# An H3-convolution and linear-attention kernel: the inverse 16-point stage by stationary products, u turned by DMA, denominators spread through DRAM

## The chip, the cores and the metric

The kernel runs on one core of a Trainium2 chip. The metric is the device time of one execution in microseconds (us), quoted as the median of several runs. The profile's span, from the first to the last instruction of the core, is about 2 us shorter. Engines are named as the profile does: PE (TensorE, matmuls), PEld (its weight loads), DVE (VectorE), ACT (ScalarE), POOL (GpSimd), SP (SyncE, which issues the DMAs here). SBUF and PSUM are the core's two on-chip memories: here matmuls write to PSUM, and an eviction is the copy of a result from there to SBUF. A turn is a transpose. A run is called slow when it is over 1.5% above the fastest run of the same kernel; some runs of about half the versions here are, the kernel before's too. Ratios and intervals use fast runs only, medians all runs.

## The reference

Two independent blocks share the output, 576 columns each, for S = 2048 rows, D = 576 and bf16 data. This is the reference cut to what matters.

```python
def A(q, k, v, shift_k, ssm_k, ssm_D):                       # H3 convolution
    kv = causal_conv_4_taps(k, shift_k) * v                  # called u in the kernel
    y  = irfft(rfft(kv padded to 2S) * rfft(ssm_k padded))[:S]
    y  = bf16(y) + kv * ssm_D
    return q * y

def B(x, wqkv, wo):                                          # linear attention, 32 heads of 18
    q, k, v = heads(x @ wqkv)
    phi = lambda t: where(t > 0, t + 1, exp(t)) + 1e-6
    num = phi(q) @ (phi(k)^T v)
    den = phi(q) . sum(phi(k)) + 1e-6
    return merge(num / den) @ wo

return concatenate([A, B], -1)
```

The kernel does the long convolution as a two-level transform: a 128-point stage with a table `Gsb`, a 16-point stage with small constant matrices, a product of the two spectra, an inverse 16-point stage, and an inverse 128-point stage with a table `Esb`. The 576 channels are worked in 9 groups of 64.

## The kernel before

Every operation is recorded with what it reads and writes. A fixed string, `PLAN`, then gives each operation's engine (P, A, D, G for GpSimd, S) and the order of issue, and another string, `PLACES`, gives the address of every tile. So the order on each engine and the sharing of memory are decided by these strings.

The inverse 16-point stage of one group. `X` is the spectrum of the filter with real and imaginary rows exchanged; the two products overwrite `xb` and `tx`. Small constant weights (64 x 64 tiles) are stationary and the products move, 512 columns a matmul; the result `V` is then turned by a DMA.

```python
load("X", xb, lambda e: dma(xb.t[0:128:2], tx.t[1:128:2]), ...)       # and the odd rows
P.op({"DVE":..., "POOL":...},                                         # the plan chooses the engine
     lambda e: vec(e).tensor_tensor(out=xb.t[:], in0=su.t[:], in1=xb.t[:], op=ALU.mult), name="p2")
P.op({"DVE":..., "POOL":...},
     lambda e: vec(e).tensor_tensor(out=tx.t[:], in0=su.t[:], in1=tx.t[:], op=ALU.mult), name="p1")
for jp in range(2):
    for wi, (w, src) in enumerate(((W31, tx), (W32, xb))):
        for h in range(2):
            for g2 in range(2):
                v = src.t[64*h:64*h+64].rearrange("p (w g) k -> p g w k", g=2)
                nc.tensor.matmul(ps.t[64*g2:64*g2+64, h, :]..., lhsT=w()[64*h:64*h+64, :],
                                 rhs=v[:, g2, 4*jp:4*jp+4, :], start=(wi == 0), stop=(wi == 1))
    copy(e, V.t[:, :, 4*jp:4*jp+4, :]..., ps.t)                       # eviction
turn("Vtr", Vt[hf].t[:, c0//4:c0//4+16, :], V.t[:]...)                # DMA transpose
```

The last stage (`i2`) reads `Vt` as the moving operand and multiplies the result by `q` on DVE:

```python
vt = Vt[hf].t[:].rearrange("p g (h r t) -> p r (g h) t", h=2, t=2)    # pairs of bf16, 128 bytes apart
nc.tensor.matmul(o, lhsT=Esb.t[:, b, ri, :], rhs=vt[:, 2*b+ri, :], start=(ri == 0), stop=(ri == 1))
nc.vector.tensor_tensor(out=qs, in0=ps.t..., in1=qs, op=ALU.mult)
```

The denominators: PE spreads the reciprocals of the heads over the heads' rows into PSUM, and DVE multiplies phi(q) by them.

```python
def b_bc(c, gp):
    ps = psb(2, "bps")
    for j in range(2):
        g = 2 * gp + j
        nc.tensor.matmul(ps.t[0:hn, j, :], lhsT=esel()[32*g:32*g+32, c, 0:hn],
                         rhs=rden.t[32*g:32*g+32, :], start=True, stop=True)
    nc.vector.scalar_tensor_tensor(out=o, in0=o, scalar=EPS, in1=ps.t[0:hn], op0=ALU.add, op1=ALU.mult)
```

The spectrum of u is turned by DVE in 32 x 32 blocks (`ct`, 9 times), the filter's by DMA (`ctH`, 9 times).

## Time and profile before

| | before |
|---|---|
| time, first three runs | 181.97 us median (181.44 to 182.95) |
| span | 180.0 us |
| PE idle in the span | 180.0 - 161.2 = 18.8 us |
| PE idle between 100 and 150 us | 50 - 21.16 - 23.44 = 5.4 us |
| DVE products at the spectrum, on DVE / on POOL | 13 / 5 |

From the page of the kernel before: the busy time of each engine, with its share of the span and its instructions, and the engines' shares of the chain that ended last.

```profile
PE 161.2 (90%) x1448; PEld 104.5 (58%) x1448; DVE 143.7 (80%) x136; ACT 109.8 (61%) x118; POOL 46.5 (26%) x29
...
PE 74%; DVE 9%; ACT 6%; DMA 6%; issue 2%; SPq 0%; DVEq 0%
```

PE is the limit: busy nine tenths of the span, and three quarters of the chain. The windows view of the kernel before gives, for each stretch, its length and the busy time (and count) of each engine, then the clock granted to PE, the share of the DMA engines and GB/s.

```profile
core 0: us, PE busy (x) PEld busy (x) DVE busy (x) ACT busy (x) POOL busy (x), PEclk, DMA share, GB/s
...
100.00:125.00 25.00, 21.16 (x239) 12.06 (x232) 22.00 (x20) 22.12 (x22) 13.77 (x4) 0.93 0.70 133
125.00:150.00 25.00, 23.44 (x259) 14.22 (x260) 22.05 (x21) 20.74 (x24) 8.88 (x2) 0.93 0.86 222
150.00:180.00 30.00, 26.36 (x172) 13.80 (x171) 20.47 (x21) 6.38 (x9) 0.00 (x0) 1.00 0.83 206
```

Three engines are nearly full in the middle, and from 150 us on PE alone. Groups of instructions, from the same kernel's lines view: count, busy us and mean ns, then the idle time before them and what ended it.

```profile
L782 DVE SCALAR_TENSOR_TENSOR pqT<-pqT,ps_all 126x1024 bf16<-126x1024 bf16 (+1 forms) x10 | 11.9, 1212 | 1.6 <-PE ps_all L776 1.4
...
L539 DVE TENSOR_TENSOR X<-spu,X 128x2048 bf16<-128x2048 bf16 x7 | 8.5, 1221 | 1.7 <-ACT spu L253 1.4 <-issue 0.3
L542 DVE TENSOR_TENSOR sph<-spu,sph 128x2048 bf16<-128x2048 bf16 x6 | 7.2, 1216 | 0.1
```

The end of the chain, from the same kernel's view of the chain (start, duration, engine, line, count), shows the two costs that the change is aimed at:

```profile
157.02 0.99 PE ps_all L553 x16
158.01 2.57 PE ps_all L795 x20
160.58 14.54 PE ps_all L581 x60
```

L553 is the inverse 16-point stage, 16 matmuls a group in 0.99 us; L581 is the last stage, 0.242 us a matmul (half of its 64 have 320 columns, half 256).

### The profile page before, as it was taken

To read this page: it belongs to the slowest core of one execution; us is meant where nothing else is said; L and a number is where in the kernel's file an instruction comes from. 1 tells how busy PE (TensorE), PEld (TensorE's weight loads), DVE (VectorE), ACT (ScalarE), POOL (GpSimd) and SP (SyncE) were. 2 spreads that over 40 slices of the span, in tenths; PEclk is the share of its full clock that TensorE was granted. 3 is DMA by queue.
4 is the path that set the end of the run, shared out by engine and by line. 5 is a ranking of instruction groups with operands and counts; after the bars stand their busy time and mean duration, and the time that the engine had idled before them with its cause. 6 is when DMAs were issued, how large, how long until landed. Compare 5 with 4: busy or idle time off the path is not lost.

```text
span 180.0 us, 3538 instructions
## 1 busy us (share of the span) xinstructions
PE 161.2 (90%) x1448; PEld 104.5 (58%) x1448; DVE 143.7 (80%) x136; ACT 109.8 (61%) x118; POOL 46.5 (26%) x29
## 2 busy tenths in 40 slices
PE   0795999999999979899999978788799999999991
PEld 0664677754766757676677745433348565554450
DVE  0307589898979899899969899996968999686863
ACT  2083364648856788755668889995958798620000
POOL 8004000150080340006304960653882000000000
PEclk9999799999999999999999999978969999999999
DMA  5999799999999944998096019979399983999844
GB/s 181 327 202 283 143 298 422 298 169 263 336 237 350 378 164 93 179 283 253 29 304 226 15 22 206 239 124 233 97 346 259 222 183 120 259 208 273 261 142 149
DMA packets 68886, 39.49 MB, mean 219 GB/s; under 512 B 50375, under 2 KB 66373, under 8 KB 68230
## 3 DMA queue, kind: packets, MB, share of 16 engines
q1 hardware_dynamic: 68870, 39.27, 84.9%
q8 instruction: 11, 0.18, 0.4%
q14 instruction: 5, 0.04, 0.1%
HBM read 17.77 MB, written 4.72 MB: 125 GB/s over the span
## 4 chain that ended last, share of the span: by engine, by line
PE 74%; DVE 9%; ACT 6%; DMA 6%; issue 2%; SPq 0%; DVEq 0%
PE ps_all L628 12%; PE ps_all L607 12%; PE ps_all L795 11%; PE ps_all L665 11%; PE ps_all L581 9%; PE ps_all L458 5%; PE ps_all L553 4%; PE ps_all L429 3%; DVE pqT L782 3%; DMA hs<-in_A_ssm_k_dram 3%; DMA wk<-in_B_wqkv_dram 3%; ACT Ch L253 2%; PE ps_all L508 2%; DVE Cu L255 2%; PE ps_all L501 2%
## 5 line engine op out<-in xcount | busy, mean ns | idle before, releaser
L407 POOL TENSOR_TENSOR v<-m,v 128x1536 bf16<-128x1536 bf16 x5 | 17.0, 3408 | 55.9 <-DVE m L404 26.2
L795 PE MATMUL ps_all<-M,pqT 126*128 126x288 bf16 (+1 forms) x160 | 24.3, 306 | 0.0
L253 ACT ACTIVATE sph<-ps_all 128x1024 bf16<-128x1024 f32 x18 | 18.0, 1022 | 8.4 <-PE ps_all L508 7.4
L607 PE MATMUL ps_all<-wk,xT 128*128 128x288 bf16 x128 | 21.4, 301 | 1.1 <-DMA wk<-in_B_wqkv_dram 1.1
L458 PEld LDWEIGHTS <-Gsb 128*128 128x128 bf16 x240 | 17.4, 102 | 7.4 <-issue 6.0
L396 DVE TENSOR_TENSOR m<-kh,Wj 128x3072 bf16<-128x3072 bf16 x12 | 20.8, 1748 | 0.9 <-DMA kh<-in_A_k_dram 0.9
L628 PE MATMUL ps_all<-xT,wq 128*126 128x512 bf16 (+1 forms) x80 | 20.7, 381 | 0.0
L665 PE MATMUL ps_all<-pk,x_sb 128*128 128x288 bf16 (+1 forms) x160 | 20.6, 287 | 0.0
L795 PEld LDWEIGHTS <-pqT 126*128 126x128 bf16 (+1 forms) x160 | 15.7, 103 | 8.3 <-issue 3.7
L253 ACT ACTIVATE spu<-ps_all 128x1024 bf16<-128x1024 f32 x16 | 15.8, 1026 | 4.9 <-PE ps_all L501 4.3
L665 PEld LDWEIGHTS <-x_sb 128*128 128x128 bf16 x160 | 15.3, 98 | 5.1 <-issue 1.3
L612 ACT ACTIVATE ek<-ps_all,neg 128x576 bf16<-128x576 f32 x16 | 11.8, 744 | 10.2 <-PE ps_all L607 5.3
L628 PEld LDWEIGHTS <-wq 128*126 128x126 bf16 (+1 forms) x100 | 12.7, 131 | 7.9 <-issue 0.9
L607 PEld LDWEIGHTS <-xT 128*128 128x128 bf16 x128 | 13.1, 103 | 5.5 <-issue 1.2
L581 PE MATMUL ps_all<-Vt,Esb 128*128 128x320 bf16 (+1 forms) x64 | 15.9, 421 | 0.0
L253 ACT ACTIVATE V<-ps_all 128x1024 bf16<-128x1024 f32 x13 | 12.9, 1022 | 4.1 <-PE ps_all L553 4.0
L632 ACT ACTIVATE eq<-ps_all,neg 126x1024 bf16<-126x1024 f32 (+1 forms) x10 | 11.1, 1112 | 6.4 <-PE ps_all L628 6.4
L586 DVE TENSOR_TENSOR q<-ps_all,q 128x640 bf16<-128x640 f32 (+1 forms) x12 | 11.2, 954 | 4.4 <-PE ps_all L581 4.4
L253 ACT ACTIVATE Ch<-ps_all 128x1536 bf16<-128x1536 f32 x9 | 13.0, 1501 | 1.8 <-PE ps_all L458 1.8
L615 DVE SCALAR_TENSOR_TENSOR pk<-ek,ps_all 128x576 bf16<-128x576 bf16 x16 | 11.8, 751 | 2.4 <-ACT ek L612 2.4
L635 DVE SCALAR_TENSOR_TENSOR pqT<-eq,ps_all 126x1024 bf16<-126x1024 bf16 (+1 forms) x10 | 12.2, 1215 | 1.7 <-ACT eq L632 1.5
L782 DVE SCALAR_TENSOR_TENSOR pqT<-pqT,ps_all 126x1024 bf16<-126x1024 bf16 (+1 forms) x10 | 11.9, 1212 | 1.6 <-PE ps_all L776 1.4
(77 smaller groups left out, 257.9 us busy)
## 6 DMA issues: line engine op xcount, KB each, us to landing
X<-sph SPq DMA_DIRECT2D x18, 256.0 KB, 3.9
hs<-in_A_ssm_k_dram SPq DMA_DIRECT2D x6, 384.0 KB, 4.1
v<-in_A_v_dram SPq DMA_DIRECT2D x2, 1152.0 KB, 9.6
x_sb<-in_B_x_dram SPq DMA_DIRECT2D x1, 2304.0 KB
out_dram<-ob SPq DMA_DIRECT2D x16, 144.0 KB, 3.1
kh<-in_A_k_dram SPq DMA_DIRECT2D x1, 1584.0 KB
q<-in_A_q_dram SPq DMA_DIRECT2D x1, 1280.0 KB
out_dram<-q SPq DMA_DIRECT2D x4, 320.0 KB, 2.6
```

The source lines that it names most:

```text
L253: nc.scalar.activation(out=o, in_=i, func=ACTF.Copy)
L396: nc.vector.tensor_tensor(out=m.t[:, i:i + 2], in0=i0, in1=i1, op=ALU.mult)
L407: lambda e: vec(e).tensor_tensor(out=vt.t[:, :, c0:c0 + CC], in0=m.t[:, 0], in1=vt.t[:, :, c0:c0 + CC], op=ALU.mult),
L458: nc.tensor.matmul(ps.t[:, bank, lo - 512 * bank:hi - 512 * bank], lhsT=Gsb.t[:, b, ri, :], rhs=src[:, lo - CC * j:hi - CC * j], start=Tru ...
L581: nc.tensor.matmul(o, lhsT=Esb.t[:, b, ri, :], rhs=vt[:, 2 * b + ri, :], start=(ri == 0), stop=(ri == 1))
L607: nc.tensor.matmul(ps.t[:, hh, 0:HALF], lhsT=xs(t, 128 * r, 128), rhs=wk.t[:, t, HALF * hh:HALF * hh + HALF], start=(t == 0), stop=(t == 4))
L612: P.op(("ACT", _act(576) + 0.085), lambda e: nc.scalar.activation(out=eb.t[:], in_=ps.t[:, :, 0:HALF], func=ACTF.Exp, bias=neg1.t[:]), rd= ...
L628: nc.tensor.matmul(ps.t[0:hn, j, :], lhsT=wq.t[:, t, h0:h0 + hn], rhs=xs(t, 1024 * gp + 512 * j, 512), start=(t == 0), stop=(t == 4))
L635: P.op(("DVE", _dve(1024)), lambda e: nc.vector.scalar_tensor_tensor(out=pqT.t[0:hn, c, 1024 * gp:1024 * gp + 1024].rearrange("p (h c) -> ...
L665: nc.tensor.matmul(ps.t[:, hh, 0:n], lhsT=x_sb.t[:, r, FT[t]:FT[t] + 128], rhs=pk.t[:, r, HALF * hh:HALF * hh + n], start=(r == 0), stop=( ...
L782: nc.vector.scalar_tensor_tensor(out=o, in0=o, scalar=EPS, in1=ps.t[0:hn], op0=ALU.add, op1=ALU.mult)
L795: nc.tensor.matmul(ps.t[:, hh, 0:HALF], lhsT=pqT.t[0:hn, c, 128 * r:128 * r + 128], rhs=M.t[0:hn, c, HALF * hh:HALF * hh + HALF], start=(c ...
```

## The change

The intent is to take work off PE and DVE. The products themselves become the stationary operand of the inverse 16-point stage and the constant matrix moves, so the result comes out already turned: the nine DMA turns of `V` go, and `Vt` gets a layout that the last stage reads in dense halves. The room on the DMA is used to turn u there in 7 of 9 groups (before on DVE), and to spread the denominators: the reciprocals go to DRAM once and come back as rows repeated 18 times, into a tile in SBUF. At the start, the first half of x is turned by PE (40 transposes) rather than by DMA. A new plan goes with it; it has 8 of the 18 products on POOL, before 5. The diff, cut to its core:

```diff
@@ inverse 16-point stage
-        V = SB("V", [128, 2, 8, 128])
...
-                            nc.tensor.matmul(
-                                ps.t[64 * g2:64 * g2 + 64, h, :].rearrange("p (w k) -> p w k", w=4),
-                                lhsT=w()[64 * h:64 * h + 64, :], rhs=v[:, g2, 4 * jp:4 * jp + 4, :],
-                                start=(wi == 0), stop=(wi == 1))
+                for j in range(8):
+                    for wi, src in enumerate((tx, xb)):
+                        nc.tensor.matmul(ps.t[:, j // 4, 128 * (j % 4):128 * (j % 4) + 128],
+                                         lhsT=src.t[:, 8 * jp + j, :], rhs=W3(wi), start=(wi == 0), stop=(wi == 1))
+            o0 = VN[hf] // 2 * jp + c0 // 2
+            ... copy(e, Vt[hf].t[:, :, o0:o0 + 32].rearrange("p r (j g) -> p j r g", g=4), ps.t...)
-        turn("Vtr", lambda: Vt[hf].t[:, c0 // 4:c0 // 4 + 16, :], ...)
@@ last stage
-                vt = Vt[hf].t[:].rearrange("p g (h r t) -> p r (g h) t", h=2, t=2)
+                vt = Vt[hf].t[:].rearrange("p r (g b t) -> p r b g t", g=2, t=2)
@@ turns of u:  groups in UT go by DMA, into the 64 x 64 second stage that the filter has
+        qt = nm == "u" and g not in UT
+UT = (1, 2, 3, 4, 5, 6, 7)
@@ denominators
+    rdd = nc.dram_tensor("rden_rows", (32, S), BF, kind="Internal").ap()
+    load("rst", RD, lambda e: dma(ap(rdd, 0, [[512, 4], [S, 32], [1, 512]]), rden.t[:]), ...)
     def b_bc(c, gp):
-        ps = psb(2, "bps")
-        ... nc.tensor.matmul(ps.t[0:hn, j, :], lhsT=esel()[32 * g:32 * g + 32, c, 0:hn], ...)
+        bt = SB("bct", [128, 2, 512])
+        load("bc", bt, lambda e: dma(bt.t[0:hn].rearrange("p h c -> p (h c)"), ap(
+            rdd, 7 * c * S + 1024 * gp, [[S, hn // 18], [0, 18], [1, 1024]])), ...)
-            nc.vector.scalar_tensor_tensor(out=o, in0=o, scalar=EPS, in1=ps.t[0:hn], op0=ALU.add, op1=ALU.mult)
+            nc.vector.scalar_tensor_tensor(out=o, in0=o, scalar=EPS, in1=bt.t[0:hn], op0=ALU.add, op1=ALU.mult)
@@ start: x loaded as it is; 40 PE transposes for rows 0 to 1023
+                        nc.tensor.transpose(out=o[:, ...], in_=x_sb.t[:, 4 * g + r, c0:c0 + 128], identity=ident())
@@ PLAN, PLACES: new
```

## The prediction

> **What bounds the kernel now.** TensorE. The page gives PE 161.2 us of a 180.0 us span (90%), DVE 143.7 (80%), ACT 109.8 (61%); 74% of the chain of work that ended last is PE. By stretches (windows view) PE idles 7.7 us of the first 17.2, 2.1 us between 62 and 100, 5.0 us between 100 and 130 (DVE 27.0 of 30 busy: DVE-bound), 0.5 us later, and 3.5 us in the tail. The granted clock is 0.87 in 17-30 and 0.88-0.89 in 115-145, after the holes: some 3-4 us more.
>
> **What the change does to PE** (spacings from the chain view):
> - Inverse 16-point stage: now 16 matmuls of 64x64 tiles, about 1.0 us a piece, 9 pieces: 9.0 us. After: 32 full weight loads with 128 columns. Full-size load+matmul pairs run here at 61-71 ns (16 transposes in 0.97-1.13 us[...]). At 60-65 ns: 288 of them = 17-19 us. **+8 to +10 us.**
> - Last stage (Esb): 60 matmuls take 14.54 us, 0.242 us each, because the moving operand is read as lone 4-byte pairs 128 bytes apart; contiguous 288-column matmuls take 0.123 us here (10 in 1.23). [...] The new layout reads dense halves in alternation: about 0.145 and 0.115 us, 64 in 8.5 us instead of 15.5. **-7 us**; DVE's product with q (12 ops, 11.2 us) then bounds the stage.
> - Denominator spreading off PE: 10 pairs of 0.4 us. **-4.1 us.**
> - u's second stage in 64x64 tiles: 0.56 against 0.38 us per piece, 7 pieces. **+1.3 us.**
> - 40 transposes of x: **+2.6 us**, but in the hole of the first 16 us.
> Net: about 0 to +2 us of PE work.
>
> **Other engines.** DVE loses 7 of 9 transposes (-8.5 us) and, to POOL, three products (-3.7); it gains 11 second-stage evictions (+13.5) against fewer first-stage (-5.3) and output ones (-4.5): about 139 us. DMA: 9 turns of Vt and 2.5 x transposes go, 7 u turns and 2.5 MB of broadcast come: about even, lighter in the first 60 us, where DMA was saturated.
>
> **Holes.** Start: k projection needs about 4.4 MB loaded first, so begins at 15-16 instead of 17.2[...]: -2 to -3 us. The first convolution tap on DVE (now at 19.0) starts 2-4 us earlier. 100-130: the PE waits on PSUM buffers and DVE fall from 5 to about 2-3 us, and 2 us of reduced clock return. Tail: unchanged, about 3.5 us.
>
> **Sum.** 182 + 1 (PE work) - 2.5 (start) - 4 (middle) - 1.5 (clock) = **175.0 us**; range 169.5 to 179.5. Faster by over 2%: 0.77; within 2%: 0.18; slower by over 2%: 0.05.
>
> **What would show it.** Inverse stage about 0.95-1.0 us per 16 matmuls, last stage 0.6 us per four of 320 columns, DVE about 139 us busy, no broadcast matmuls, k projection at 15-16 us, PE idle 100-130 under 3 us. Wrong: last-stage spacing still near 0.24 us; DMA waits of PE or DVE for u turns or broadcasts.
>
> **What would make it wrong.** Alternating 4-byte reads could be as slow as lone ones (+7 us, no gain left). The SP queue is in order: a turn waiting for its eviction delays all issues behind it. [...] If all holes outside start and tail close: 170.

The marked cuts took out figures and warnings that no trace of this case shows. The start's -2 to -3 us: from 17.2 to 15 or 16 us is only 1.2 to 2.2. Three figures are estimates from the trace of the kernel before: 15 to 16 us for 4.4 MB (that is 275 to 293 GB/s; its DMA moved 276 between 17.2 and 30 us and 286 between 30 and 60), 0.145 and 0.115 us for the last stage's matmuls (from 0.123 us for 288 contiguous columns), and what the clock would give back (from 0.87 in 17-30 and 0.89 in 115-145; that it returns when holes close is not shown). That the DMA was saturated in the first 60 us is its share of 1.01 there. That the SP queue is in order shows in the changed kernel's trace: the turn at 110.35 us held it for 7.23 us, 6.7 of them by the waits view waiting for DVE, and the load of rows behind it was issued at 117.68.

## More of the kernel before

The denominators' product, L782, takes 1.21 us each. It does so also while POOL works on a product, as the timeline of the kernel before shows (start, duration, engine, line):

```profile
116.52 4.83 DVE L782 SCALAR_TENSOR_TENSOR pqT<-pqT,ps_all 126x1024 bf16<-126x1024 bf16 x4
...
119.13 4.06 POOL L542 TENSOR_TENSOR sph<-spu,sph 128x2048 bf16<-128x2048 bf16 x1 [2.86 <-ACT spu L253]
```

Four of them in 4.83 us, though POOL's product starts in the middle of them. Three others start while a POOL product is already under way (at 105.59, 128.02 and 129.79) and take 1.18 to 1.22 us as well.

## The result, and the profile after

The time rose: 194.14 us median (193.27 to 194.86, four fast runs) against 182.46 (181.44 to 183.35, four runs) of the kernel before. The ratio is 1.064, with a 95% interval of 1.0559 to 1.0721. A ratio is the mean time of one kernel's fast runs over that of the other's of the same rounds, so it is not quite the ratio of the medians quoted.

From the page of the changed kernel, the same lines as before:

```profile
PE 159.8 (83%) x1556; PEld 117.7 (61%) x1556; DVE 160.3 (84%) x134; ACT 109.0 (57%) x116; POOL 60.9 (32%) x34
...
PE 45%; DVE 23%; DMA 12%; ACT 6%; POOL 5%; issue 4%; SPq 3%; DVEq 0%; ACTq 0%; POOLq 0%
```

PE's work did not grow: 159.8 us busy against 161.2. Its idle time did, to 191.6 - 159.8 = 31.8 us from 18.8. DVE has 160.3 us busy where 139 were predicted, and its share of the chain went from 9% to 23%; the denominators' product alone has 8% of the chain (L814), before 3% (L782). The windows view of the changed kernel says where:

```profile
100.00:125.00 25.00, 16.58 (x192) 13.13 (x188) 22.37 (x14) 17.67 (x16) 16.98 (x4) 0.86 0.77 136
125.00:150.00 25.00, 16.72 (x129) 9.97 (x130) 24.18 (x15) 10.94 (x14) 15.68 (x4) 0.84 1.03 214
150.00:180.00 30.00, 28.11 (x342) 20.84 (x341) 25.68 (x22) 18.90 (x22) 4.38 (x2) 0.96 0.64 197
```

Between 100 and 150 us PE is idle 16.7 us, before 5.4. DVE is busy almost throughout, yet with 29 instructions where it had 41. The lines view of the changed kernel names the group:

```profile
L814 DVE SCALAR_TENSOR_TENSOR pqT<-pqT,bct 126x1024 bf16<-126x1024 bf16 (+1 forms) x10 | 28.9, 2908 | 1.1 <-DMA bct<-rden_rows 1.0
...
L583 DVE TENSOR_TENSOR sph<-spu,sph 128x2048 bf16<-128x2048 bf16 x6 | 8.3, 1390 | 0.1
L580 DVE TENSOR_TENSOR X<-spu,X 128x2048 bf16<-128x2048 bf16 x4 | 7.8, 1960 | 0.0
```

The same instruction on the same shape takes 2.9 us instead of 1.21. It waits for nothing that the idle columns show: 1.1 us of waits in all ten. The two DVE products are longer too. At 1.21 us an instruction the three groups would take 28.9 + 8.3 + 7.8 - 20 x 1.21 = 20.8 us less, and DVE would stand at 139.5: the figure predicted. The timeline of the changed kernel, DVE's lines beside POOL's, shows what stretches them:

```profile
107.94 4.08 POOL L583 TENSOR_TENSOR sph<-spu,sph 128x2048 bf16<-128x2048 bf16 x1
...
108.20 4.90 DVE L814 SCALAR_TENSOR_TENSOR pqT<-pqT,bct 72x1024 bf16<-72x1024 bf16 x1 [1.02 <-DMA bct<-rden_rows]
...
115.82 1.21 DVE L814 SCALAR_TENSOR_TENSOR pqT<-pqT,bct 126x1024 bf16<-126x1024 bf16 x1
...
116.12 4.83 POOL L583 TENSOR_TENSOR sph<-spu,sph 128x2048 bf16<-128x2048 bf16 x1 [4.11 <-issue]
...
117.62 4.42 DVE L814 SCALAR_TENSOR_TENSOR pqT<-pqT,bct 126x1024 bf16<-126x1024 bf16 x1
...
132.93 5.98 POOL L580 TENSOR_TENSOR X<-spu,X 128x2048 bf16<-128x2048 bf16 x1 [6.96 <-ACT spu L254]
...
133.80 1.17 DVE L814 SCALAR_TENSOR_TENSOR pqT<-pqT,bct 126x1024 bf16<-126x1024 bf16 x1
...
135.72 9.26 DVE L814 SCALAR_TENSOR_TENSOR pqT<-pqT,bct 126x1024 bf16<-126x1024 bf16 x2
...
138.86 5.04 POOL L583 TENSOR_TENSOR sph<-spu,sph 128x2048 bf16<-128x2048 bf16 x1
```

Six of the ten start while a POOL product is under way, and five of these end about 1.1 us after POOL: at 113.10 (POOL 112.02), 122.04 (POOL 120.95), one that starts at 122.63 (not shown), and the pair, whose second ends at 144.98 (POOL 143.90). The one at 115.82, which started while POOL was free, took its 1.21 us. So it seems to stand still for as long as POOL's instruction runs, and then to do its own work. In the kernel before, with the second operand in PSUM, it did not. One case went the other way: at 133.80 POOL's product had been under way since 132.93, yet DVE's took 1.17 us and POOL's 5.98, which is 1.9 more than the 4.08 of the first one shown. There POOL seems to have been the one that stood; why, the trace does not say.

The start did not gain: the first k-projection matmul begins at 18.70 us in the chain of the changed kernel, before at 17.23.

### The profile page after: what moved, and what is told of

Its sections match the earlier page's. It is cut to its first block, busy times and chain, and to the rows that moved or that the text cites. A ratio compares the mean times of both kernels' runs of the same rounds, so it can differ in the third digit from the quotient of the medians.

```text
span 191.6 us, 3755 instructions
## 1 busy us (share of the span) xinstructions
PE 159.8 (83%) x1556; PEld 117.7 (61%) x1556; DVE 160.3 (84%) x134; ACT 109.0 (57%) x116; POOL 60.9 (32%) x34
## 4 chain that ended last, share of the span: by engine, by line
PE 45%; DVE 23%; DMA 12%; ACT 6%; POOL 5%; issue 4%; SPq 3%; DVEq 0%; ACTq 0%; POOLq 0%
PE ps_all L698 8%; PE ps_all L663 8%; DVE pqT L814 8%; DMA bct<-rden_rows 6%; PE ps_all L642 5%; PE ps_all L827 5%; PE ps_all L616 5%; PE ps_all L498 4%; DMA ctH<-Ch 4%; DVE X L580 3%; PE ps_all L591 3%; ACT Cu L254 2%; PE ps_all L549 2%; SPq L246 2%; PE ps_all L468 2%
## 5 line engine op out<-in xcount | busy, mean ns | idle before, releaser
L580 POOL TENSOR_TENSOR X<-spu,X 128x2048 bf16<-128x2048 bf16 x5 | 23.2, 4645 | 31.6 <-DMA X<-sph 13.7
L814 DVE SCALAR_TENSOR_TENSOR pqT<-pqT,bct 126x1024 bf16<-126x1024 bf16 (+1 forms) x10 | 28.9, 2908 | 1.1 <-DMA bct<-rden_rows 1.0
L827 PE MATMUL ps_all<-M,pqT 126*128 126x288 bf16 (+1 forms) x160 | 24.3, 307 | 2.9 <-DVE pqT L814 2.9
L827 PEld LDWEIGHTS <-pqT 126*128 126x128 bf16 (+1 forms) x160 | 15.9, 103 | 11.4 <-DVE pqT L814 3.5
L549 PE MATMUL ps_all<-ctH,cst 64*64 64x512 bf16 x128 | 12.6, 449 | 10.8 <-DVE sph L256 5.2
L591 PE MATMUL ps_all<-cst,sph 128*128 128x128 bf16 x144 | 17.5, 220 | 2.3 <-DVE sph L583 1.7
L254 ACT ACTIVATE ob<-ps_all 128x576 bf16<-128x576 f32 x14 | 9.0, 651 | 17.1 <-PE ps_all L827 9.0
L254 ACT ACTIVATE sph<-ps_all 128x1024 bf16<-128x1024 f32 x13 | 13.1, 1024 | 9.4 <-PE ps_all L549 9.4
L254 ACT ACTIVATE Vt<-ps_all 128x1024 bf16<-128x1024 f32 x14 | 14.0, 1031 | 7.6 <-PE ps_all L591 7.6
L698 PEld LDWEIGHTS <-x_sb 128*128 128x128 bf16 x160 | 15.5, 98 | 4.1 <-issue 0.2
L591 PE MATMUL ps_all<-cst,X 128*128 128x128 bf16 x144 | 17.4, 220 | 0.0
L591 PEld LDWEIGHTS <-sph 128*128 128x128 bf16 x144 | 14.2, 99 | 3.1 <-DVE sph L583 2.1
L254 ACT ACTIVATE Cu<-ps_all 128x1536 bf16<-128x1536 f32 x10 | 14.8, 1514 | 1.0 <-PE ps_all L498 1.0
```

The source lines that it names most:

```text
L254: nc.scalar.activation(out=o, in_=i, func=ACTF.Copy)
L549: nc.tensor.matmul(ps.t[64 * h:64 * h + 64, r, :].rearrange("p (b k) -> p b k", b=4), lhsT=W2D()[64 * r:64 * r + 64, :], rhs=cv[64 * r:64 ...
L591: nc.tensor.matmul(ps.t[:, j // 4, 128 * (j % 4):128 * (j % 4) + 128], lhsT=src.t[:, 8 * jp + j, :], rhs=W3(wi), start=(wi == 0), stop=(wi ...
L698: nc.tensor.matmul(ps.t[:, hh, 0:n], lhsT=x_sb.t[:, r, FT[t]:FT[t] + 128], rhs=pk.t[:, r, HALF * hh:HALF * hh + n], start=(r == 0), stop=( ...
L827: nc.tensor.matmul(ps.t[:, hh, 0:HALF], lhsT=pqT.t[0:hn, c, 128 * r:128 * r + 128], rhs=M.t[0:hn, c, HALF * hh:HALF * hh + HALF], start=(c ...
```

## The experiments

The theory, A: the denominators' product now has two operands in SBUF, and such a DVE instruction stands still while POOL's product, which reads SBUF too, runs. What speaks for it so far is above: five of the six that start during a POOL product end about 1.1 us after it, where in the kernel before, with one operand in PSUM, four took 4.83 us beside one. That the place of the operand decides was a conjecture, which e1, d1 and e2 test. Below, this is called the lock. The rivals: B, the rows come late from DRAM and the DMA queue is what costs; C, the start; D, the new inverse stage costs more than the last stage saves; E, u's turns on the DMA.

Unless said otherwise every kernel gave the right result, and each set of runs has its own runs of the kernel before on the same chip (medians 181.8 to 182.8 us). Sixteen kernels ran.

### e1: the eight POOL products to DVE

An edit of the plan alone: in eight tokens the G becomes a D.

```diff
- G403 G404 G416 G417 G437 G438 G450 G510
+ D403 D404 D416 D417 D437 D438 D450 D510
```

> Changed kernel with its 8 products on POOL moved to DVE; nothing else. Theory A (lock: DVE instructions with two SBUF operands stand still while a POOL tensor op runs; the change made the denominators' product such an instruction): the denominators' product falls from 2.9 to about 1.17 us each, products on DVE all at 1.22, DVE busy 160 - 21 + 10 = about 149 us, time about 184-187 us. Rival B (the round trip of the denominators through DRAM, the in-order queue and the late u turns cost the time; the long DVE instructions are a by-product of slow memory): DVE gets 10 us more work, so time 194 us or more, and the product stays over 2 us. Rival C (a slow start, TensorE from 6.4 us): time within 1% of 194.

186.24 us median (185.92 to 186.6), ratio 1.0242 (1.0157 to 1.0327): 8 us of the 12 come back although DVE took on eight products (by the ratios, 4.0 of the 6.4 points). From the lines view of e1:

```profile
L814 DVE SCALAR_TENSOR_TENSOR pqT<-pqT,bct 126x1024 bf16<-126x1024 bf16 (+1 forms) x10 | 12.0, 1218 | 5.8 <-DMA bct<-rden_rows 5.8
...
L580 DVE TENSOR_TENSOR X<-spu,X 128x2048 bf16<-128x2048 bf16 x9 | 10.9, 1211 | 0.0
```

The instruction is back at 1.218 us with the same operands in the same places, and DVE's busy time fell from 160.3 to 148.3 us. What is left are waits for the rows (5.8 us), and 2.4%. The edit removes two things at once, the lock and the slower products on POOL (4.6 us each in the changed kernel); d2 is for the second.

### d1: the lock in the kernel before

The reverse test: the kernel before keeps its plan and its broadcast matmuls, but the product reads 1024 columns of the table `Gsb` instead of PSUM. Its output is wrong, which doesn't matter for the time.

```diff
-  nc.vector.scalar_tensor_tensor(out=o, in0=o, scalar=EPS, in1=ps.t[0:hn], op0=ALU.add, op1=ALU.mult)
+  nc.vector.scalar_tensor_tensor(out=o, in0=o, scalar=EPS, in1=Gsb.t[0:hn, 0:4, :, :]..., op0=ALU.add, op1=ALU.mult)
```

> Kernel before, wrong result on purpose: the denominators' product takes its second operand from a table in SBUF instead of PSUM; nothing else differs, the broadcast matmuls stay. Theory A: those of the 10 products that meet one of POOL's products stand still until it ends; in the trace of before 3 to 5 do, so mean rises from 1.21 to 2-2.5 us and time grows by 3-8 us. Rival B: no change in time (no DRAM trip was added); the product slightly faster, 1.17 us.

189.73 us (189.27 to 190.4), ratio 1.0436 (1.0344 to 1.0528). From its lines view:

```profile
L782 DVE SCALAR_TENSOR_TENSOR pqT<-pqT,Gsb 126x1024 bf16<-126x1024 bf16 (+1 forms) x10 | 23.5, 2383 | 0.0
```

The place of one operand alone, with nothing else of the change, doubles the mean of the instruction and costs 4.4%. There is no trip through DRAM here and no new stage. With e1, theory A is shown in both directions: 2.908 to 1.218 us there, 1.212 to 2.383 here.

### d2: the products to DVE in the kernel before

A control for e1: perhaps POOL was merely slow. Five tokens of the kernel before's plan change from G to D.

```diff
- G388 G402 G424 G437 G451
+ D388 D402 D424 D437 D451
```

> The kernel before with its five products on GpSimd moved to VectorE, the same move that gained 8 us in the changed kernel. If GpSimd is simply too slow for the products, whatever else runs, the move gains here as well: 179 to 181.5. If the gain there came from freeing VectorE's two-operand instruction from GpSimd, there is little to free here, because the denominators' product reads PSUM, and VectorE only takes on 5 times 1.22 = 6.1 us more in its busiest stretch: 182 to 185. The denominators' product should then read 1.21 us as before, and the products on VectorE 1.22 us each.

185.96 us median, but two of the four runs were slow; the two fast ones are 181.98 and 183.65, ratio 1.0126 (0.999 to 1.0261). The move that gained 8 us in the changed kernel shows no gain here. POOL's slowness as such was not the trouble in this kernel.

### e2: the broadcast back on PE, the POOL products left

The denominators' rows come from PSUM again; the ten `bc` operations become pairs of matmuls placed where the plan's PSUM had room.

```diff
-        bt = SB("bct", [128, 2, 512])
-        load("bc", bt, ... rdd ...)
+        bt = psb(2, "bps")
+        ... nc.tensor.matmul(bt.t[0:hn, j, :], lhsT=esel()[32 * g:32 * g + 32, c, 0:hn], rhs=rden.t[...])
```

> Changed kernel with the spreading of the denominators put back on PE, so that the product reads PSUM and SBUF as in the kernel before; POOL's products stay. Theory A: the product falls from 2.9 to 1.21 us while POOL runs, 17 us of DVE time come back, PE gets 4 us of matmuls: time about 182-186. Rival B predicts a gain too, but through vanished DMA waits, of about the 3-6 us between denominators and first product. Rival C: within 1% of 194.

192.01 us median (three fast runs 190.85 to 192.89, one slow), ratio 1.0538 (1.0407 to 1.0668). From its lines view:

```profile
L819 DVE SCALAR_TENSOR_TENSOR pqT<-pqT,ps_all 126x1024 bf16<-126x1024 bf16 (+1 forms) x10 | 12.2, 1216 | 11.6 <-PE ps_all L813 11.6
...
L583 DVE TENSOR_TENSOR sph<-spu,sph 128x2048 bf16<-128x2048 bf16 x6 | 10.9, 1823 | 0.1
```

The lock is gone from the product, with POOL still working beside it, as A says. The DVE products with two SBUF operands are still held up (1.82 us, against 1.22 in the kernel before). The time gained little because DVE now waited 11.6 us for the matmuls: PSUM is packed by the plan, and each pair could only be put just ahead of its use. The gain was turned into a new wait, so e2's time is a miss, and only its durations count.

### e3 and e7: the start

In the changed kernel the first matmul waits until 6.45 us for a memset of `ones` on POOL, behind eight others. e3 puts it first in the changed kernel; e7 does so in e5 (below).

```diff
- G13 S22 S7 G1 S36 G0 G27 ... S50 G28 G8 S21 G160
+ G8 G13 S22 S7 G1 S36 G0 G27 ... S50 G28 S21 G160
```

> Changed kernel with one memset (the row of ones that the first matmuls need) put first on POOL instead of behind eight others. Theory A: the start is a side matter; first matmul at 3-4 us instead of 6.4, k projection up to 2 us earlier, time 192-194. Rival C (the start holds the loss): 3 us or more gained.

> The run with early broadcast loads, and the ones memset first on POOL. Alone in the changed kernel the memset moved the time by less than 1%; the same is expected here: within 1% of the run without it.

e3: 193.69 us median, two of four runs slow; the fast ones 191.11 and 193.29. The k projection began at 18.45 us by its chain instead of 18.70. e7: 185.61 us (185.47 to 186.85), ratio 1.0258 (1.0156 to 1.0359), against e5's 1.0256. The memset is not where the time went: in e3 the first matmul starts at 4.53 us, 1.9 earlier, and the k projection only 0.25 earlier. In the changed kernel, first-stage matmuls stand ahead of the k projection and wait for a DVE eviction until 17.21 us. The rest of the start (C) has no run of its own.

### e4: u turned by DVE again, on e1

```diff
-UT = (1, 2, 3, 4, 5, 6, 7)
+UT = ()
- S396 S409 S443 S430 S477 S456 S490
+ D396 D409 D443 D430 D477 D456 D490
```

> Changed kernel with products on DVE (186.2 us) and u's seven DMA turns taken back to DVE transposes. If the u turns by DMA pay (they free 8.5 us of DVE), this is slower than 186 by 2-6 us; if their latency and their place in the in-order queue cost more than they free, the broadcast loads behind them come early, DVE's DMA waits fall from 5.8 us to under 2, and the time is 182-185.

185.61 us (184.29 to 186.23), ratio 1.0233 (1.0119 to 1.0347), the same as e1's 1.0242. DVE's waits for the rows fall to 1.2 us, but DVE is 8 us busier (156.0). Neither expectation came true: the waits fell, and the time stayed. On e1, turning u by DMA (E) is neither a loss nor a gain.

### e5 and the two e13: the rows' place in the queue, on e1

The DMAs that bring the rows stand in SyncE's queue behind turns that hold it for several us each (in e1 7.80 us from 110.10 and 3.82 from 118.82, a load of rows behind each). e5 issues three of the ten loads earlier.

```diff
- S214 D196 S208 A353 ... S218 D476 P412 S430 P356 ... P199 D213 S210 P354 ... P191 S206 A198 ... P407 S202 A192
+ S214 D196 S208 S206 S202 A353 ... S218 D476 P412 S210 S430 P356 ... P199 D213 P354 ... P191 A198 ... P407 A192
```

> Changed kernel with products on DVE (186.2 us), and three of the four late broadcast loads issued ahead of the u turns that held them up in the in-order queue (two of them into other places in SBUF). If the queue order is a cost on the critical path: DVE's waits for broadcast loads fall from 5.8 to under 2.5 us and the time to 182-184. If TensorE's holes there come from evictions and PSUM instead: waits fall, time within 1% of 186.

186.16 us (185.24 to 186.62), ratio 1.0256 (1.0136 to 1.0376). The waits for the rows moved and grew to 9.1 us in three, one of them 7.9 us; both expectations had them fall, so this is a miss. The two others leave the order and issue all ten loads from another engine, POOL (idle there since e1) or ACT.

```diff
- S216 S204 S212 S214 S208 S218 S210 S206 S202 S220
+ G216 G204 G212 G214 G208 G218 G210 G206 G202 G220
-  dma(bt.t[0:hn]..., ap(rdd, ...))
+  nc.gpsimd.dma_start(out=bt.t[0:hn]..., in_=ap(rdd, ...))
```

> e1 with the ten loads of the denominators' rows issued from GpSimd, which is idle then, instead of SyncE's queue. The same bytes move. If VectorE's 5.8 us of waits for them came of their place in the queue behind turns that hold it 2 to 8 us each, the waits go below 2 us and the time falls by 2 to 5 us: 181 to 184. If the DMA engines were simply full, the waits stay and so does the time: 185.5 to 187.

> As the run before it, with the ten loads issued from ScalarE. If the queue was the cause: 181 to 185, less good than from GpSimd [...]. If the DMA engines were full: 185.5 to 188.

From POOL: 185.48 us (183.88 to 187.07, one slow), ratio 1.0255 (1.0062 to 1.0448). From ACT: 188.5 us, ratio 1.0442 (1.0296 to 1.0589), just above both ranges. On this chip only two of the seven runs of the kernel before count as fast (179.37 and 181.33; the others are at 182.09 to 183.56), so the ratios of e11, e12 and the two e13 rest on those two; by the medians of all runs the POOL version stands at 185.48 / 182.29 = 1.018. The waits view of the POOL version between 95 and 150 us (what waited for what: us, times, longest):

```profile
DVE pqT L814 <- DMA bct<-rden_rows: 6.3, 2, 3.5
```

Off the queue that the turns hold, the waits are as large as on it (5.8 us in e1); in the ACT version they are 3.6 us, and the time is longer. So no run shows that the place in that queue (B in this form) costs. That the DMA engines are full there would fit, their share being 1.00 between 120 and 150 us in the POOL version, but these runs moved no fewer bytes. In e4, which took seven turns off the DMA, the waits did fall.

### e6: the new inverse stage alone, in the kernel before

The diff of the inverse and last stage shown above, applied to the kernel before with its own plan; the nine turns of `V` go, the constant matrix gets a tile of its own, and the first piece of the first group moves a little back to where its tile is free.

```diff
-            turn("Vtr", ...)                     # nine S tokens leave the plan
+    W3t = SB("W3t", [128, 256]);  load("W3t", W3t, ...)
+    ... lhsT=src.t[:, 8 * jp + j, :], rhs=W3(wi) ...
```

> Kernel before with the first part of the change alone: products as stationary operand, Vt written by the evictions, its nine DMA turns gone; denominators, u and x as before; the first piece's inverse stage a little later, for want of SBUF. By the spacings measured in the changed kernel PE gets 18.9 - 9.0 = +9.9 us in the inverse stage and 9.4 - 15.5 = -6.1 us in the last one, net +3.8 us, against turns taken out of the tail: 182-187 us. If this part held the loss instead of the lock: 190 or more. If it is what the change should have gained by: under 180.

186.35 us (186.05 to 188.89, one slow), ratio 1.0278 (1.0165 to 1.0391). From the chain of e6:

```profile
162.58 1.79 PE ps_all L552 x32
164.37 0.68 PE ps_all L577 x4
...
169.29 3.42 PE ps_all L577 x20
```

A group of the inverse stage now takes 1.79 us (before 0.99), 56 ns a matmul with its weight load; that is 9 x 0.80 = 7.2 us more. The last stage takes 0.170 us for a matmul of 320 columns instead of 0.270, and 0.137 instead of 0.218 for 256 columns (median spacings in the traces of e6 and the kernel before); over its 64 matmuls it took 0.75 + 2.72 + 6.41 = 9.9 us in e1's chain against 1.17 + 14.54 = 15.7 before, 5.8 us less. So by its matmuls at full clock (granted 1.00 from 140 us on in e6 and the kernel before, 0.99 from 150 on in e1) the swap adds 1.4 us. The span of e6 is 4.1 us longer than before: PE's busy time, 163.8 us, is 2.6 above the kernel before, and its idle time 1.5. A part of the busy time is the clock, which was 0.66 between 120 and 130 us of that profile and 0.84 in the kernel before. So D is right in this kernel: the swap alone costs time, and more than its matmuls do. Why the rest came with it is not shown.

### e9: e6 with its last stretch in another order

In e6 DVE's products with q run back to back at the end. e9 moves four steps of the last stage up among the earlier work, puts two output projections between the last ones, and gives three output evictions to ACT (the expectation speaks of one; the plan that ran has A219, A234 and A240). PE's operations in order:

```diff
- P490 P230 P470 P472 P248 P221 P483 P485 P503 P496 P498 P239 P218 P513 P511 P508 P516 P501 P518 P506 P528 P522 P531 P525 P233
+ P490 P230 P503 P470 P513 P472 P248 P511 P221 P483 P485 P508 P496 P498 P516 P501 P518 P239 P506 P528 P218 P522 P531 P525 P233
- D219 D234 D240
+ A219 A234 A240
```

> This is e6 (the kernel before with the new inverse stage alone) with its last stretch in another order: four of the eight i2 steps of the first half move up between the s2 and i1 work, two output projections move in among the last i2 steps, and one of the last output evictions goes to ScalarE. If e6's 3.5 us over the kernel before are a tail in which VectorE multiplies by q back to back while TensorE has run dry, this order takes 2 to 3.5 us of it back: 183 to 184 against e6's 186.35. If they are TensorE work (16-row to 128-row products cost more than the smaller i2 saves, 2.6 us more busy time), TensorE is busy throughout from 140 us on in e6 too and the order gives 0 to 1 us: 185.3 to 186.5.

189.79 us median with two slow runs; fast 187.89 and 188.79, ratio 1.0431 (1.031 to 1.0553). Neither theory had it slower. PE did not gain in work (163.2 us), it waited more, and the last stores landed later. It is a miss: it shows only that this order is worse, and that e6's loss isn't cured by spreading these products. It agrees with a count that needs no run: from 140 us on PE had 39.74 us of work in e6 and 36.23 in the kernel before, so with no idle time from there on e6 would still have ended about 3.5 us later. Of these, 2.6 are its longer busy time as a whole, and 0.9 is work that it had not yet done at 140 us.

### e8 and e10: everything but the lock and the new stage

If e1's remaining 2.4% were the new inverse stage, e1 with the old stage put back should be as fast as the kernel before. e8 does this, e10 turns u on DVE as well.

```diff
+        V = SB("V", [128, 2, 8, 128])
+        turn("Vtr", ...)                          # nine S tokens more, each after its second eviction
-UT = (1, 2, 3, 4, 5, 6, 7)                         # e10 only
+UT = ()
```

> This is e1 (the changed kernel with its products on VectorE, so without the lock) with the inverse stage of before put back: 32-wide stationary weights, the nine turns by DMA, and only the first piece of group 0 moved beside its second. What is left of the change is u turned by DMA, the denominators' trip through DRAM and the start. If e1's remaining loss of 2.4% is the new inverse stage, as e6 says, it goes away: 180.5 to 183.5, ratio 0.99 to 1.01, with TensorE's busy time 3 us under e1's. If it lies in the trip through DRAM or the turns of u, it stays: 185 to 187, ratio 1.02 to 1.03.

> e8 with u turned on VectorE again, so that the DMA turns are 18 as in the kernel before and no longer 25. What is left of the change is the denominators' trip through DRAM and the start with some x turned on TensorE; all products are on VectorE as in d2. If e8's 34 us were the queue of DMA turns (each holds the issuing queue for 2 to 2.5 us and waits there for its source), they go: 182 to 187, and if e1's remaining loss is the new inverse stage the ratio is 1.00 to 1.015, like d2's. If the trip through DRAM or the changed start costs those 3 to 4 us, it is 1.02 to 1.03. Above 1.05, this order of work is simply bad for the queue and says nothing of either.

e8: 216.95 us, ratio 1.2009 (1.1895 to 1.2122). e10: 211.12 us, ratio 1.1544 (1.1503 to 1.1586). Both are misses. The plan was made for an inverse stage that needs no turn; with it, `V` waits for turns and PE for `Vt` (in e10's waits view ACT waits 6.0 us for turns before it writes `V`, and PE 13.5 us for `Vt`). The timeline of SyncE's queue in e8 shows what one turn takes of it:

```profile
126.23 2.05 SPq L513 DMA_TRANSPOSE Vt<-V  x1
128.34 2.48 SPq L513 DMA_TRANSPOSE ctH<-Ch  x1
130.91 0.75 SPq L245 DMA_DIRECT2D bct<-rden_rows  x1
```

So a turn holds the queue for 2.05 and 2.48 us here, a plain load for 0.75; in the changed kernel the turns into `ctH` take 1.6 to 9.2 us of it, waits included. But e10, with 18 turns as in the kernel before, is only 6 us better than e8 with 25, so the number of turns is at most a small part of it (e10's expectation said what it would then tell: nothing of the parts). In this plan the new inverse stage could not be undone by itself.

### e11 and e12: e1 without the trip through DRAM

e11 is e1 and e2 together: products on DVE, broadcast on PE. e12 turns u on DVE as well, so that the new inverse stage and the start are what is left of the change.

```diff
- G403 G404 G416 G417 G437 G438 G450 G510     # from e2
+ D403 D404 D416 D417 D437 D438 D450 D510
-UT = (1, 2, 3, 4, 5, 6, 7)                     # e12 only, with seven S tokens to D
+UT = ()
```

> e1 (products on VectorE) and e2 (denominators spread by TensorE into PSUM again) together: no lock, no trip through DRAM; u is still turned by DMA and the inverse stage is the new one. TensorE gets 4.3 us of work back. If e1's 5 us of new holes are the trip through DRAM, they close and the sum is about even or better: 181.5 to 184.5, ratio 1.00 to 1.01. If they are the new inverse stage or the turns of u, the 4.3 us come on top or hide in the holes: 186 to 189, ratio 1.02 to 1.04.

> e11 with u turned by VectorE again: what is left of the change is the new inverse stage, the start and the products on VectorE. DMA traffic falls by 7 turns. If the turns of u held the queue and the DMA engines, this is faster than e11 by 2 us or more; if VectorE, which takes 8.5 us more, bounds the middle, it is slower than e11 by 1 to 3 us. If the new inverse stage alone costs 3.5 us (e6) whatever else is there, it stays at 185 or above.

e11: 189.32 us median (fast 187.84 to 190.09, one slow), ratio 1.0511 (1.0363 to 1.0659). e12: 193.43 us (192.04 to 194.38), ratio 1.0719 (1.0561 to 1.0878). Taking away the trip through DRAM in this way makes e1 slower, not faster: given this plan's PSUM the trip is the better of the two ways. As in e2, DVE waits for the just-in-time broadcasts (9.2 us in e11's profile, which was a slow run), so neither says what a plan made for PSUM broadcasts could do, nor what the trip costs in e1.

No version tried beats the kernel before. The best of the changed kernel's are e13 from POOL, e4 and e7, at 185.5 to 185.6 us.

## Why the prediction was wrong

The prediction was 175.0 us (169.5 to 179.5); 194.14 us came. Point by point:

- **"DVE about 139 us busy": the step that failed.** It was 160.3. The figure was right for the instructions as such, for without the stretching DVE stands at 139.5; there was some luck in it, since the terms that the prediction lists add up to 143.7 - 8.5 - 3.7 + 13.5 - 5.3 - 4.5 = 135.2. What was missed is that the denominators' product, by moving its second operand from PSUM to SBUF, came under POOL's lock, in the same change that gave POOL three more products. The prediction counted those three as a saving ("and, to POOL, three products (-3.7)"). The runs show it in both directions: e1 takes 7.9 us back with the lock, and d1 puts the lock alone into the kernel before and loses 4.4%.
- **"100-130: the PE waits on PSUM buffers and DVE fall from 5 to about 2-3 us": wrong for the same reason.** Between 100 and 130 PE was idle 30 - 18.63 = 11.4 us, and between 100 and 150 it was 16.7, before 5.4. By the waits view of that stretch PE waited 2.9 us for the product itself (L827), and 5.2 + 4.8 us for evictions on DVE, the engine that the product held (L549). With the lock gone this part still didn't gain: in e1 PE is idle 11.0 us between 95 and 150 (55 - 19.50 - 24.55 in its windows view), before 5.6. No version got the -4 us.
- **"2 us of reduced clock return", -1.5 us in the sum: wrong.** The clock was 0.86 and 0.84 in the two stretches, before 0.93. That this follows from the holes is not shown: between 95 and 150 us the e13 from POOL has 11.8 us of them and a clock of 0.94, the kernel before 5.6 and the same 0.94. Early on it did return: between 17.2 and 30 us it was 1.00, before 0.87.
- **PE work "about 0 to +2 us": near, a little high.** 159.8 us against 161.2. The parts were near too: the last stage 9.9 instead of 15.7 us in e1 (predicted 8.5 instead of 15.5), the weight-load pairs of the inverse stage 56 ns at full clock (predicted 60 to 65). But it says little of the swap by itself: the swap alone costs 2.8% (e6), and in the sum the four us of broadcast matmuls that left PE offset its extra matmul time.
- **The dense halves: right in kind, a little short in size.** Reads in alternation were not as slow as lone pairs (0.170 against 0.270 us at 320 columns; predicted 0.145). By the column that is 0.84 ns for lone pairs, 0.53 for dense halves in alternation, and 0.43 for a contiguous operand (L795, 288 columns in 0.123 us). The old pairs lay 128 bytes apart. In the new layout the pairs of a half lie side by side, but the reads alternate between two halves 320 or 256 bytes apart.
- **Start, -2.5 us: wrong.** The k projection began at 18.70 us, not at 15 to 16; it begins behind first-stage matmuls that wait for an eviction, not behind its loads. The first convolution tap on DVE did start earlier, at 17.08 instead of 18.99 us. Moving the memset did not mend it (e3, e7).
- **What the prediction named as dangers** is not what lost the 8 us: the queue order and DMA waits for the turns of u. Changing these two on e1 (e5, e13, e4) gained nothing.

What stays open: e1's remaining 2.4%, about 4 us. Other places in the queue (e5, e13), turning u on DVE (e4) and an earlier memset (e7) did not bring it back. The trip through DRAM is not excluded: in e1's chain 9.0% of the span is the landing of the rows, and e11 only traded it for other waits; against it speaks e4, where the waits for the rows fall to 1.2 us and the time stays. The new inverse stage costs as much in the kernel before, which makes it a likely cause, but only 1.4 us of that are its matmuls, and putting the old stage back into e1 gave a kernel too slow to tell (e8, e10). That it is this stage is argued, not shown.

## What to carry to other kernels

Before moving an operand of a VectorE instruction from PSUM to SBUF, count its SBUF inputs: with two of them it stood still here while GpSimd multiplied from SBUF (2.9 us on the mean instead of 1.21, 2.38 in d1), so the move and the work given to GpSimd must be judged together. Look for it in the durations, not in the waits: the instruction is shown as busy, with the same shape and a mean that has doubled, and its end follows the end of a GpSimd instruction by about its own normal time (1.1 us, in five of six). And undoing one part of a change inside a plan made for the whole may say little (e2, e8, e10, e11); the part put alone into the kernel before (d1, e6) was the better test here.
